# Loading x, k and v rows in longer runs and reordering the weight folds at the start of a gated attention/FFN kernel

## The chip, the cores and the metric

The kernel runs on one core of one Trainium2 chip. The metric is the device time of one execution in microseconds (us). All executions told here are of the state "fast", with a granted TensorE clock of 0.998 to 1.0 in the run records.

## The reference

```python
def reference(x, wqkv, w_phi, wo, w_gate, w_up, w_down, gate_w):   # cut: names of A and B merged
    g = sigmoid((x * gate_w).sum(-1, keepdims=True))
    # a: linear attention with softmax features, 32 heads of 20
    q, k, v = split(x @ wqkv)                       # x [2048, 640], wqkv [640, 1920]
    pq, pk = q @ w_phi[h], k @ w_phi[h]             # per head, 20 x 20
    phi_q = concat(softmax(pq), softmax(-pq)); phi_k = the same of pk
    kv, z = phi_k^T v, sum(phi_k)                   # over all rows
    a = (phi_q kv / (phi_q z + 1e-6)) @ wo
    b = (gelu(x @ w_gate) * (x @ w_up)) @ w_down    # inner width 1728
    return g * a + (1 - g) * b
```

## The kernel before

The rows of x are worked on in 16 tiles of 128; four tiles make a block. The kernel does not compute k and then multiply it by w_phi. It folds w_phi into the weights first: `wk2 = Wk * blockdiag(w_phi)`, and the same for q. For this it needs Wk and Wq transposed (`wkT`, `wqT`). Wk is transposed on TensorE. Wq is transposed by six DMA-transpose loads. Only the first four tiles of x pass through this start; from tile 4 on a steady loop runs, whose first instruction is the first v projection with 512 columns. I call it **the full projection** and use its start time as the milestone for everything that comes before.

Two words recur. A bank is one of the eight pieces (0 to 7) of the memory into which matmuls write their results. An eviction is the copy of a bank's content into a weight or data tile by VectorE or ScalarE; until it is done, the program lets no later matmul write that bank.

The loads (cut):

```python
xload(0, "sp"); xload(2, "act"); xload(1, "sp"); xload(3, "act")     # x of block 0, one tile each
for kt in range(KD):                                                  # v rows, five loads
    sc.dma("sp", ... self.wvk[:, kt, 0:D] <- w3[:, kt, 2*D:3*D], writes=[("wv", kt)])
sc.dma("act", ... wphi ...)                                           # 640 runs of 40 bytes
sc.dma("sp", ... self.wk_raw <- w3[:, :, D:2*D], writes=["wk_raw"])   # k rows, one load
sc.dma("sp", gload, writes=["wgate"])                                 # gate_w as a column: 640 runs of 2 bytes
for g, (h0, nh) in enumerate(self.GH):                                # six transposed loads of Wq
    sc.dma("sp", ... dma_start_transpose(self.wqT[:, g, :], ...),
           reads=["wk_raw"] if g == 0 else [], writes=[("wqT", g)])
xblock(1); xblock(2); xblock(3)                                       # transposed x of the other blocks
# ... FFN weights follow
```

One fold is six small matmuls and one eviction, by VectorE ("d") or ScalarE ("a"):

```python
def fold(self, kt, which, banks, ekey):
    for g, (h0, nh) in enumerate(self.GH):
        # matmul into banks[h0 // 16], reads ("w%sT" % which, g) and the block diagonal
    # one copy of both banks to wk2[kt] or wq2[kt] by VectorE or ScalarE

def pq(self, b, i, n):          # q projection: 5 matmuls into bank 6 + n % 2, the kt-th reads wq2[kt]
```

The order of the start (cut):

```python
for t, ek in enumerate("adad"): self.x_transpose(t, 4 + t, ek)     # banks 4..7
self.v_first({... blockdiag and first k transposes inside ...})    # v of tiles 0..3
self.w_transposes("k", (2, 3, 4, 5), (0, 6, 7, 0), "dadd")
for kt, (bk, ek) in enumerate(zip((6, 1, 4, 6, 0), "adada")):
    self.fold(kt, "k", (bk, bk + 1), ek)
self.k_early(0, 2)                    # k projection of tile 0, banks 2 and 3
self.k_early(1, 4)
self.fold(0, "q", (6, 7), "d"); self.fold(1, "q", (0, 1), "a")
self.k_early(2, 2)
self.fold(2, "q", (6, 7), "d"); self.fold(3, "q", (0, 1), "a"); self.fold(4, "q", (6, 7), "d")
self.k_norm(0)                        # softmax normalisation of k tile 0, VectorE
self.k_early(3, 4)
self.k_norm(1)
self.pq(0, 1, 1); self.pq(0, 0, 0); self.pq(0, 3, 3)
self.gram(0)                          # phi_k^T v of tile 0
self.k_norm(2)
self.pq(0, 2, 2)
# steady loop: vk(t), k_norm(t), gram, pq for t = 4..15, then the FFN
```

The softmax here doesn't subtract the row's maximum and nothing guards it: scores larger than these inputs give would overflow.

## Time and profile before

| | us |
|---|---|
| timed executions beside the first profile | 307.12, 307.26, 307.62 |
| the profiled execution itself | 306.63 |
| its span | 304.70 |
| first v matmul / first q fold / first q projection / full projection | 6.93 / 20.39 / 25.46 / 30.96 |

In the lines of the profile PE is TensorE, PEld its weight loads, DVE VectorE, ACT ScalarE, POOL GpSimd and SP SyncE, which sends out most loads (SPq is its queue); L345 is line 345 of that kernel's file. The head and the engine line of the page of the kernel before (busy time, share of the span, instructions):

```profile
span 304.7 us, 5022 instructions
...
PE 298.0 (98%) x2011; PEld 175.3 (58%) x2011; DVE 160.0 (53%) x312; ACT 106.8 (35%) x189; POOL 29.8 (10%) x59
```

TensorE is the limit. In this trace a fold matmul has a length of 0.21 us while the next one starts 0.05 us after it, so gaps of 0.15 us and less do not show as idle time; I count from start to start. The next lines are TensorE's waits in the kernel before between 4 and 32 us (engine, what was waiting, what released it: total us, times, longest).

```profile
PE ps L345 <- DVE wq_50 L358: 0.7, 1, 0.7
PE ps L376 <- DMA wvk<-in_A_wqkv_dram: 0.6, 1, 0.6
PE ps L488 <- ACT Eq L494: 0.3, 1, 0.3
PE ps L345 <- ACT wvk L360: 0.3, 1, 0.3
PE ps L365 <- DVE wvk L358: 0.2, 1, 0.2
```

TensorE waits for the first v rows, and several times for evictions that free a bank or deliver folded weights. These are lines of the timeline of the kernel before (start, length, engine, line, operation, count; in brackets the idle time before it and its releaser):

```profile
10.63 8.33 SPq L227 DMA_TRANSPOSE wqT<-in_A_wqkv_dram  x6
...
20.39 0.77 PE L345 MATMUL ps<-BD,wqT 120*128 120x120 bf16 x12
21.00 1.53 PE L365 MATMUL ps<-wvk,xT 128*128 128x384 bf16 x10
22.36 0.76 PE L345 MATMUL ps<-BD,wqT 120*128 120x120 bf16 x12
23.80 0.46 PE L345 MATMUL ps<-BD,wqT 120*128 120x120 bf16 x6 [0.68 <-DVE wq_50 L358]
24.10 1.53 PE L365 MATMUL ps<-wvk,xT 128*128 128x384 bf16 x10
25.46 2.32 PE L488 MATMUL ps<-xT,wq_50 128*128 128x512 bf16 x10
28.12 1.25 PE L488 MATMUL ps<-xT,wq_50 128*128 128x512 bf16 x5 [0.34 <-ACT Eq L494]
```

### The profile page before, as it was taken

Reading aid. Unit: us, or ns where it says so; the run is one execution under the profiler, and the core shown is the slowest. Engines: PE = TensorE matmul, PEld = TensorE weight load, DVE = VectorE, ACT = ScalarE, POOL = GpSimd, SP = SyncE. Lnnn points to the kernel's source line nnn. Section 1 sums busy time; section 2 is a strip of 40 time slices with the busy share of each in tenths; the row PEclk is TensorE's granted clock in tenths of the full one; section 3 lists DMA queues with packets and bytes.
Section 4 is the critical chain, followed back from the end, with each engine's and each line's share of the span. In section 5 each row is a group of like instructions: output and inputs, shape, how many; then the busy total and the mean of one; then the engine's idle time right before and its main releaser. Section 6 shows DMA issues by size and latency. Waiting matters only on the chain.

```text
span 304.7 us, 5022 instructions
## 1 busy us (share of the span) xinstructions
PE 298.0 (98%) x2011; PEld 175.3 (58%) x2011; DVE 160.0 (53%) x312; ACT 106.8 (35%) x189; POOL 29.8 (10%) x59
## 2 busy tenths in 40 slices
PE   7998999999999999999999999999999999999996
PEld 4664565655555555677545567754457764545763
DVE  1438999586775877234367710435770044567000
ACT  3388666667674222111322211123221122222111
POOL 7100000000000011111011000101110010111000
PEclk9999999999999999999999999999999999999999
DMA  7589996000000011120120111011111001110401
GB/s 222 140 150 209 369 369 221 0 2 0 2 0 0 2 22 24 24 65 25 43 20 4 22 24 43 24 43 23 17 6 44 24 26 41 22 22 0 45 22 45
DMA packets 34641, 18.29 MB, mean 60 GB/s; under 512 B 25850, under 2 KB 34618, under 8 KB 34618
## 3 DMA queue, kind: packets, MB, share of 16 engines
q1 hardware_dynamic: 33680, 17.62, 22.8%
q10 hardware_dynamic: 938, 0.35, 0.4%
q8 instruction: 16, 0.26, 0.4%
q14 instruction: 7, 0.06, 0.1%
HBM read 9.78 MB, written 2.62 MB: 41 GB/s over the span
## 4 chain that ended last, share of the span: by engine, by line
PE 94%; DMA 2%; ACT 1%; DVE 1%; issue 0%; SPq 0%; ACTq 0%; DVEq 0%
PE ps L572 37%; PE ps L654 20%; PE ps L365 12%; PE ps L660 7%; PE ps L488 6%; PE ps L609 4%; PE ps L462 4%; PE ps L376 2%; DMA wvk<-in_A_wqkv_dram 2%; PE ps L582 1%; PE ps L345 1%; ACT Eq L494 1%; PE ps L327 0%; ACT Ek L423 0%; DVE wkT L334 0%
## 5 line engine op out<-in xcount | busy, mean ns | idle before, releaser
L572 PE MATMUL ps<-xT,wu_sb 128*128 128x512 bf16 x260 | 64.6, 379 | 0.2 <-ACT Eq L494 0.2
L572 PE MATMUL ps<-xT,wg_sb 128*128 128x512 bf16 x260 | 64.6, 379 | 0.0
L654 PE MATMUL ps<-wd_sb,hT 128*128 128x320 bf16 (+2 forms) x448 | 63.8, 299 | 0.0
L575 ACT ACTIVATE gl<-ps 128x512 bf16<-128x512 f32 x52 | 31.1, 597 | 83.2 <-PE ps L572 81.0
L577 DVE TENSOR_TENSOR hT<-ps,gl 128x512 bf16<-128x512 f32 x52 | 35.7, 688 | 42.9 <-PE ps L572 42.9
L654 PEld LDWEIGHTS ps<-wd_sb,hT 128*128 128x128 bf16 x448 | 43.1, 98 | 18.2 <-DVE hT L577 0.4
L572 PEld LDWEIGHTS ps<-xT,wu_sb 128*128 128x128 bf16 x260 | 25.4, 98 | 31.1 <-issue 0.7
L365 PE MATMUL ps<-wvk,xT 128*128 128x512 bf16 (+2 forms) x220 | 40.6, 335 | 0.2 <-DVE wvk L358 0.2
L572 PEld LDWEIGHTS ps<-xT,wg_sb 128*128 128x128 bf16 x260 | 24.9, 98 | 26.9
L670 ACT ACTIVATE outsb<-ps,Gm 128x640 bf16<-128x640 f32 (+2 forms) x17 | 13.0, 763 | 74.1 <-PE ps L660 74.1
L638 POOL TENSOR_TENSOR Og<-O_59,O_60 128x640 bf16<-128x640 bf16 x16 | 22.3, 1396 | 167.8 <-DVE O_60 L636 167.8
L365 PEld LDWEIGHTS ps<-wvk,xT 128*128 128x128 bf16 x220 | 21.1, 97 | 19.5 <-DVE wvk L358 0.6
L434 DVE TENSOR_REDUCE Dk<-Ek 128x64 f32<-128x1280 bf16 x16 | 23.7, 1482 | 10.0 <-ACT gcol L426 10.0
L625 DVE RECIPROCAL RH<-ps 128x32 f32<-128x32 f32 x16 | 5.7, 358 | 43.9 <-PE ps L609 42.8
L443 DVE TENSOR_TENSOR Ek<-Ek,Dk 128x640 bf16<-128x640 bf16 x32 | 25.0, 822 | 0.5
L488 PE MATMUL ps<-xT,wq_50 128*128 128x512 bf16 x100 | 24.7, 378 | 0.3 <-ACT Eq L494 0.3
L660 PE MATMUL ps<-wo_sb,goT 128*128 128x320 bf16 (+2 forms) x160 | 24.5, 299 | 0.0
L494 ACT ACTIVATE Eq<-ps 128x512 bf16<-128x512 f32 x40 | 21.8, 607 | 5.4 <-PE ps L488 5.4
L423 ACT ACTIVATE Ek<-ps 128x640 bf16<-128x640 f32 x32 | 20.7, 703 | 2.2 <-PE ps L365 2.2
L660 PEld LDWEIGHTS ps<-wo_sb,goT 128*128 128x128 bf16 x160 | 15.5, 98 | 6.3
L609 PEld LDWEIGHTS ps<-KV,Eq 128*128 128x128 bf16 x192 | 12.0, 98 | 3.1
L609 PE MATMUL ps<-KV,Eq 128*128 128x154 bf16 x192 | 13.7, 221 | 0.0
(68 smaller groups left out, 178.7 us busy)
## 6 DMA issues: line engine op xcount, KB each, us to landing
out_dram<-outsb SPq DMA_DIRECT2D x15, 160.0 KB, 1.8
wd_sb<-in_B_w_down_dram SPq DMA_DIRECT2D x1, 2080.0 KB, 12.7
wg_sb<-in_B_w_gate_dram SPq DMA_DIRECT2D x1, 1120.0 KB, 7.0
wu_sb<-in_B_w_up_dram SPq DMA_DIRECT2D x1, 1120.0 KB, 9.5
wg_sb<-in_B_w_gate_dram SPq DMA_DIRECT2D x1, 960.0 KB, 9.0
wu_sb<-in_B_w_up_dram SPq DMA_DIRECT2D x1, 960.0 KB, 9.4
wvk<-in_A_wqkv_dram SPq DMA_DIRECT2D x5, 160.0 KB, 4.8
wk_raw<-in_A_wqkv_dram SPq DMA_DIRECT2D x1, 800.0 KB, 6.5
```

The costliest lines, as they stand in the source:

```text
L365: sc.op("pe", lambda e, kt=kt: e.matmul(self.bank(bank)[:, bcol:bcol + n], self.xT[:, kt, t * P:(t + 1) * P], self.wvk[:, kt, c0:c0 + n], ...
L434: sc.op("dve", lambda e: e.tensor_reduce(self.Dk[:, se, 0, :].rearrange("p (s h) -> p s h", h=H), self.Ek[:, se, :, :].rearrange("p s (h d ...
L443: sc.op("dve", lambda e, v=v, r=r: e.tensor_tensor(v, v, r, ALU.mult), reads=[("Rk", se)], writes=[("Ek", se, s)])
L488: sc.op("pe", lambda e, kt=kt: e.matmul(self.bank(bank), self.wq2[:, kt, i * P:(i + 1) * P], self.xT[:, kt, b * self.BT:(b + 1) * self.BT] ...
L494: sc.op("act", lambda e, s=s, scale=scale: e.activation(self.Eq[:, s, i, b * self.BT:(b + 1) * self.BT], self.bank(bank), AF.Exp, scale=sc ...
L572: sc.op("pe", lambda e, kt=kt, w=w, bk=bk: e.matmul(self.bank(bk), w[:, kt, c * P:(c + 1) * P], xs(kt), start=(kt == 0), stop=(kt == self. ...
L575: sc.op("act", lambda e: e.activation(self.gl[:, slot, :], self.bank(banks[0]), AF.Gelu_apprx_tanh), reads=[("ps", banks[0])], writes=[("g ...
L577: sc.op("dve", lambda e: e.tensor_tensor(self.hT[:, c, :], self.bank(banks[1]), self.gl[:, slot, :], ALU.mult), reads=[("ps", banks[1]), ( ...
L609: sc.op("pe", lambda e, s=s, i=i, n=n, o0=o0, k0=k0, bk=bk, r=r: e.matmul(self.bank(bk)[:, o0:o0 + n], self.Eq[:, s, i, t * P:(t + 1) * P] ...
L638: sc.op("pool", lambda e: e.tensor_tensor(self.Og[:, sl, :], self.O1[:, sl, :], self.O2[:, sl, :], ALU.add), reads=[("O", 0, sl), ("O", 1, ...
L654: sc.op("pe", lambda e: e.matmul(self.bank(bk, w), self.hT[:, c, tt * P:(tt + 1) * P], self.wd_sb[:, c, w0:w0 + w], start=(c == 0), stop=F ...
L660: sc.op("pe", lambda e: e.matmul(self.bank(bk, w), self.goT[:, gs, k, :], self.wo_sb[:, k, w0:w0 + w], start=False, stop=(k == self.KD - 1 ...
```

## The change

Its intent is to fill TensorE's gaps at the start. Loads: x of block 0 goes in two loads of two tiles (2560-byte runs; the rows of block 0 are dealt out differently, and its stores follow); k and v rows come as one run per k-slice; the gate column comes as one row and is turned by five tiny matmuls. Order: v steps and k transposes interleaved differently, k folds over three bank pairs with k of tile 0 between them, q folds between the k tiles and all evicted by VectorE.

```diff
-        xload(0, "sp"); xload(2, "act"); xload(1, "sp"); xload(3, "act")        # condensed
-        for kt in range(KD): ... wvk[:, kt, 0:D] <- v rows
-        ... wk_raw <- k rows; gload (gate column)
+        xload(2, "act")                               # tiles 2 and 3
+        sc.dma("act", ... wphi ...); sc.dma("act", ... gw_row ...)
+        xload(0, "sp")                                # tiles 0 and 1
+        for kt in range(KD): ... w3[:, kt, 0:2*D] <- k and v rows, writes=[("wv", kt), ("wk", kt)]
@@ order
+        warm(7); xt(0, 6, "a"); xt(1, 7, "d"); warm(2); xt(2, 6, "a"); xt(3, 7, "d")
+        vs(0, 0); vs(1, 0); self.gate_column(3); vs(2, 0); vs(3, 0)
+        ... v steps, blockdiag, k transposes tk(0..5) between the last v steps ...
+        self.fold(0, "k", (6, 7), "d")
+        self.fold(1, "k", (4, 5), "a")
+        self.fold(2, "k", (2, 3), "d")
+        ks(0, 0)                                      # k of tile 0, one k-slice
+        self.fold(3, "k", (6, 7), "a")
+        ks(0, 1)
+        self.fold(4, "k", (4, 5), "d")
+        ks(0, 2); ks(0, 3); ks(0, 4)
+        self.k_evac(0, 0)
+        self.k_early(1, 2)
         self.fold(0, "q", (6, 7), "d")
-        self.fold(1, "q", (0, 1), "a")
-        self.k_early(2, 2)
+        self.fold(1, "q", (0, 1), "d")
+        self.k_early(2, 4)
         self.fold(2, "q", (6, 7), "d")
-        self.fold(3, "q", (0, 1), "a")
+        self.fold(3, "q", (0, 1), "d")
+        self.k_early(3, 2)
         self.fold(4, "q", (6, 7), "d")
         self.k_norm(0)
-        self.k_early(3, 4)
         self.k_norm(1)
         self.pq(0, 1, 1)
```

(Several calls stand on one line here; the cuts are marked.)

More of the change, by code (lines that the diff above doesn't have):

```diff
@@ L157, in alloc @@
         self.zero = T("zero", [P, 512], BF16)
+        self.gw_row = T("gw_row", [1, D], BF16)
+        self.one = T("one", [1, 1], BF16)
         self.gcol = T("gcol", [P, NT], F32)
@@ L186, in alloc @@
         place([
-            [("wvk", [P, KD, 2 * D + 2], BF16), ("wq2", [P, KD, D], BF16)],
+            [("w3", [P, KD, 3 * D + 2], BF16), ("wq2", [P, KD, D], BF16)],
             [("hT", [P, NFC, BT], BF16), ("gl", [P, 3, BT], BF16)],
@@ L190, in alloc @@
         place([
-            [("xtok", [P, self.TB, D], BF16), ("wk_raw", [P, KD, D], BF16),
-             ("wkT", [P, 6, D], BF16), ("wqT", [P, 6, D], BF16), ("wq_raw", [P, KD, D], BF16)],
+            [("xtok", [P, self.TB, D], BF16), ("wkT", [P, 6, D], BF16), ("wqT", [P, 6, D], BF16)],
             [("goT", [P, 6, KD, P], BF16), ("O1", [P, 2, D], BF16), ("O2", [P, 2, D], BF16),
@@ L208, in loads @@
         w3 = self.wqkv.rearrange("(kt p) n -> p kt n", p=P)
-        def gload(e):
-            with nc.allow_non_contiguous_dma(reason="gate_w as a column"):
-                return e.dma_start(self.wvk[:, :, 2 * D:2 * D + 1], self.gw.rearrange("(kt p o) -> p kt o", p=P, o=1))
-        def xload(t, q):
-            sc.dma(q, lambda e: e.dma_start(self.xtok[:, t, :], self.x[t * P:(t + 1) * P, :]), writes=[("xtok", t)])
-        xload(0, "sp")
+        x4 = self.x[0:self.BT, :].rearrange("(p j) n -> p j n", j=self.TB)
@@ L216, in loads, with xload, kvload @@
+        def xload(j, q):
+            sc.dma(q, lambda e: e.dma_start(self.xtok[:, j:j + 2, :], x4[:, j:j + 2, :]),
+                   writes=[("xtok", j), ("xtok", j + 1)])
+        def kvload(kt):
+            sc.dma("sp", lambda e: e.dma_start(self.w3[:, kt, 0:2 * D], w3[:, kt, D:3 * D]), writes=[("wv", kt), ("wk", kt)])
         xload(2, "act")
-        xload(1, "sp")
-        xload(3, "act")
-        for kt in range(KD):
-            sc.dma("sp", lambda e, kt=kt: e.dma_start(self.wvk[:, kt, 0:D], w3[:, kt, 2 * D:3 * D]), writes=[("wv", kt)])
@@ L221, in loads @@
         sc.dma("act", lambda e: e.dma_start(self.wphi_sb[:, :].rearrange("d (h f) -> d h f", f=DH),
                                             self.wphi.rearrange("h d f -> d h f")), writes=["wphi"])
-        sc.dma("sp", lambda e: e.dma_start(self.wk_raw[:, :, :], w3[:, :, D:2 * D]), writes=["wk_raw"])
-        if self.QDMA:
-            sc.dma("sp", gload, writes=["wgate"])
-            for g, (h0, nh) in enumerate(self.GH):
-                sc.dma("sp", lambda e, g=g, h0=h0: e.dma_start_transpose(
-                    self.wqT[:, g, :], self.wqkv[:, h0 * DH:h0 * DH + P]),
-                    reads=["wk_raw"] if g == 0 else [], writes=[("wqT", g)])
-        else:
-            sc.dma("sp", lambda e: e.dma_start(self.wq_raw[:, :, :], w3[:, :, 0:D]), writes=["wq_raw"])
-            sc.dma("sp", gload, writes=["wgate"])
+        sc.dma("act", lambda e: e.dma_start(self.gw_row[0:1, :], self.gw.rearrange("(o n) -> o n", o=1)), writes=["gw_row"])
@@ L234, in xblock @@
+        xload(0, "sp")
+        for kt in range(KD):
+            kvload(kt)
+        for g, (h0, nh) in enumerate(self.GH):
+            sc.dma("sp", lambda e, g=g, h0=h0: e.dma_start_transpose(
+                self.wqT[:, g, :], self.wqkv[:, h0 * DH:h0 * DH + P]),
+                reads=[("wk", KD - 1)] if g == 0 else [], writes=[("wqT", g)])
         def xblock(b, after=()):
@@ L237, in xblock @@
                 reads=after, writes=[("xT", t) for t in range(b * 4, b * 4 + 4)])
-        xblock(1, [] if self.QDMA else ["wq_raw"])
+        xblock(1)
         xblock(2)
@@ L317, in blockdiag, with wk_transposes @@
             reads=rd, writes=["BD"])
-    def w_transposes(self, which, gs, banks, ekeys):
+    def wk_transposes(self, gs, banks, ekeys):
         sc = self.sc
-        raw, T = (self.wk_raw, self.wkT) if which == "k" else (self.wq_raw, self.wqT)
         for g, b, ek in zip(gs, banks, ekeys):
@@ L327, in w_transposes, with gate_column @@
                 sc.op("pe", lambda e, kt=kt: e.transpose(
-                    pv[0:rows, kt * P:(kt + 1) * P], raw[:, kt, h0 * self.DH:h0 * self.DH + rows], self.ident[:, :]),
-                    reads=["w%s_raw" % which, "ident"], writes=[("ps", b)], signal=(kt == self.KD - 1))
-            dst = T[0:rows, g, :]
+                    pv[0:rows, kt * P:(kt + 1) * P], self.w3[:, kt, h0 * self.DH:h0 * self.DH + rows],
+                    self.ident[:, :]),
+                    reads=[("wk", kt), "ident"], writes=[("ps", b)], signal=(kt == self.KD - 1))
+            dst = self.wkT[0:rows, g, :]
             src = pv[0:rows, 0:self.D]
-            wr = [("w%sT" % which, g)]
             if ek == "d":
-                sc.op("dve", lambda e: e.tensor_copy(dst, src), reads=[("ps", b)], writes=wr)
+                sc.op("dve", lambda e: e.tensor_copy(dst, src), reads=[("ps", b)], writes=[("wkT", g)])
             else:
-                sc.op("act", lambda e: e.activation(dst, src, AF.Copy), reads=[("ps", b)], writes=wr)
+                sc.op("act", lambda e: e.activation(dst, src, AF.Copy), reads=[("ps", b)], writes=[("wkT", g)])
+    def gate_column(self, b):
+        sc = self.sc
+        for kt in range(self.KD):
+            sc.op("pe", lambda e, kt=kt: e.matmul(
+                self.bank(b)[:, kt:kt + 1], self.gw_row[0:1, kt * P:(kt + 1) * P], self.one[0:1, 0:1],
+                start=(kt == 0), stop=(kt == self.KD - 1), skip_group_check=True),
+                reads=["gw_row", "one"], writes=[("ps", b)], signal=(kt == self.KD - 1))
+        sc.op("dve", lambda e: e.tensor_copy(
+            self.w3[:, :, 3 * self.D:3 * self.D + 1], self.bank(b, self.KD).unsqueeze(2)),
+            reads=[("ps", b)], writes=["wgate"])
     def fold(self, kt, which, banks, ekey):
@@ L350, in fold @@
         if which == "k":
-            dst = self.wvk[:, kt, self.D:2 * self.D]
+            dst = self.w3[:, kt, 2 * self.D:3 * self.D]
         else:
@@ L365, in proj @@
             sc.op("pe", lambda e, kt=kt: e.matmul(
-                self.bank(bank)[:, bcol:bcol + n], self.xT[:, kt, t * P:(t + 1) * P], self.wvk[:, kt, c0:c0 + n],
+                self.bank(bank)[:, bcol:bcol + n], self.xT[:, kt, t * P:(t + 1) * P], self.w3[:, kt, self.D + c0:self.D + c0 + n],
                 start=(kt == 0), stop=(kt == self.KD - 1)),
@@ L369, in proj, with v_step, k_step @@
                 writes=[("ps", bank)], signal=(kt == self.KD - 1))
-    def v_first(self, extra):
+    def v_step(self, t, kt):
         sc = self.sc
-        for kt in range(self.KD):
-            for t in range(4):
-                for c0, n, bk, col in ((0, 480, t, 0), (480, 160, 4 + t // 3, 160 * (t % 3))):
-                    sc.op("pe", lambda e, kt=kt, t=t, c0=c0, n=n, bk=bk, col=col: e.matmul(
-                        self.bank(bk)[:, col:col + n], self.xT[:, kt, t * P:(t + 1) * P], self.wvk[:, kt, c0:c0 + n],
-                        start=(kt == 0 and col == 0), stop=(kt == self.KD - 1), skip_group_check=True),
-                        reads=[("xT", t), ("wv", kt)], writes=[("ps", bk)], signal=(kt == self.KD - 1))
-                for f in extra.get((kt, t), ()):
-                    f()
+        for c0, n, bk, col in ((0, 480, t, 0), (480, 160, 4 + t // 3, 160 * (t % 3))):
+            sc.op("pe", lambda e, c0=c0, n=n, bk=bk, col=col: e.matmul(
+                self.bank(bk)[:, col:col + n], self.xT[:, kt, t * P:(t + 1) * P], self.w3[:, kt, self.D + c0:self.D + c0 + n],
+                start=(kt == 0 and col == 0), stop=(kt == self.KD - 1), skip_group_check=True),
+                reads=[("xT", t), ("wv", kt)], writes=[("ps", bk)], signal=(kt == self.KD - 1))
+    def k_step(self, t, kt):
+        sc = self.sc
+        for c0, n, bk, col in ((640, 384, 2 * t, 128), (1024, 257, 2 * t + 1, 0)):
+            sc.op("pe", lambda e, c0=c0, n=n, bk=bk, col=col: e.matmul(
+                self.bank(bk)[:, col:col + n], self.xT[:, kt, t * P:(t + 1) * P], self.w3[:, kt, self.D + c0:self.D + c0 + n],
+                start=(kt == 0), stop=(kt == self.KD - 1)),
+                reads=[("xT", t), ("wk2", kt), "wgate"], writes=[("ps", bk)], signal=(kt == self.KD - 1))
     def v_first_evac(self, ts, ek, tail):
@@ L510, in attention_state @@
         order = [(b, i) for b in range(self.NB) for i in range(self.KD)]
-        self.sc.op("dve", lambda e: e.memset(self.zero[:, :], 0.0), writes=["zero"])
-        for i in range(self.NWARM):
-            self.sc.op("pe", lambda e: e.matmul(self.bank(3), self.zero[:, 0:P], self.zero[:, :], start=True, stop=True),
-                       reads=["zero"], writes=[("ps", 3)])
-        for t, ek in enumerate("adad"):
-            self.x_transpose(t, 4 + t, ek)
-        tk = lambda g, b, ek: (lambda: self.w_transposes("k", (g,), (b,), ek))
@@ L518, in attention_state @@
-        ve = lambda ts, ek, tail=False: (lambda: self.v_first_evac(ts, ek, tail))
-        self.v_first({(1, 3): [lambda: self.blockdiag((6, 7))],
-                      (4, 0): [ve([0], "a")],
-                      (4, 1): [tk(0, 6, "d"), ve([1], "a")],
-                      (4, 2): [tk(1, 7, "d"), ve([2], "a")]})
-        self.w_transposes("k", (2, 3, 4, 5), (0, 6, 7, 0), "dadd")
-        ve([0, 1, 2], "a", True)()
-        ve([3], "a")()
-        ve([3], "a", True)()
-        for kt, (bk, ek) in enumerate(zip((6, 1, 4, 6, 0), "adada")):
-            self.fold(kt, "k", (bk, bk + 1), ek)
@@ L529, in attention_state, with warm @@
-        self.k_early(0, 2)
-        self.k_early(1, 4)
+        sc = self.sc
+        sc.op("dve", lambda e: e.memset(self.zero[:, :], 0.0), writes=["zero"])
+        sc.op("dve", lambda e: e.memset(self.one[:, :], 1.0), writes=["one"])
+        def warm(n):
+            for i in range(n):
+                sc.op("pe", lambda e: e.matmul(self.bank(3), self.zero[:, 0:P], self.zero[:, :], start=True, stop=True),
+                      reads=["zero"], writes=[("ps", 3)])
+        vs, ve, xt = self.v_step, self.v_first_evac, self.x_transpose
@@ new lines, in attention_state @@
+        tk = lambda g, b, ek: self.wk_transposes((g,), (b,), ek)
+        warm(7)
+        xt(0, 6, "a")
+        xt(1, 7, "d")
+        warm(2)
+        xt(2, 6, "a")
+        xt(3, 7, "d")
+        vs(0, 0)
+        vs(1, 0)
+        self.gate_column(3)
+        vs(2, 0)
+        vs(3, 0)
+        for t in range(4):
+            vs(t, 1)
+        self.blockdiag((6, 7))
+        for kt in (2, 3):
+            for t in range(4):
+                vs(t, kt)
+        tk(0, 6, "d")
+        tk(1, 7, "a")
@@ new lines, in attention_state @@
+        vs(0, 4)
+        ve([0], "a", False)
+        vs(1, 4)
+        tk(2, 6, "d")
+        ve([1], "a", False)
+        vs(2, 4)
+        tk(3, 7, "d")
+        ve([2], "a", False)
+        vs(3, 4)
+        tk(4, 0, "d")
+        tk(5, 1, "d")
+        ve([0, 1, 2], "a", True)
+        ve([3], "a", False)
+        ve([3], "a", True)
+        ks = self.k_step
+        self.fold(0, "k", (6, 7), "d")
+        self.fold(1, "k", (4, 5), "a")
+        self.fold(2, "k", (2, 3), "d")
+        ks(0, 0)
@@ L531, in attention_state @@
+        self.fold(3, "k", (6, 7), "a")
+        ks(0, 1)
+        self.fold(4, "k", (4, 5), "d")
+        ks(0, 2)
+        ks(0, 3)
+        ks(0, 4)
+        self.k_evac(0, 0)
+        self.k_early(1, 2)
         self.fold(0, "q", (6, 7), "d")
-        self.fold(1, "q", (0, 1), "a")
-        self.k_early(2, 2)
+        self.fold(1, "q", (0, 1), "d")
+        self.k_early(2, 4)
         self.fold(2, "q", (6, 7), "d")
-        self.fold(3, "q", (0, 1), "a")
+        self.fold(3, "q", (0, 1), "d")
@@ L595, in num @@
         DB, DH = self.DB, self.DH
-        old = [("xtok", k) for k in range(4)] + ["wk_raw"] + [("wkT", g) for g in range(6)] + [("wqT", g) for g in range(6)] + ["wq_raw"]
+        old = [("xtok", k) for k in range(4)] + [("wkT", g) for g in range(6)] + [("wqT", g) for g in range(6)]
         parts = {0: [(0, 0, 6), (1, 6, 12), (2, 12, 15)], 1: [(2, 16, 19), (3, 19, 25), (4, 25, 31)]}
@@ L671, in evac @@
                   reads=[("ps", k) for k in bks] + ["Gm"], writes=[("outsb", os_, w)for w in ((0, 320) if n == 640 else (w0,))])
-            sc.dma("sp", lambda e: e.dma_start(self.out[t * P:(t + 1) * P, w0:w0 + n], self.outsb[:, os_, w0:w0 + n]),
+            rows = self.out[t * P:(t + 1) * P, :]
+            if t < self.TB:
+                rows = self.out[0:self.BT, :].rearrange("(p j) n -> p j n", j=self.TB)[:, t, :]
+            sc.dma("sp", lambda e: e.dma_start(rows[:, w0:w0 + n], self.outsb[:, os_, w0:w0 + n]),
                    reads=[("outsb", os_, w) for w in ((0, 320) if n == 640 else (w0,))], writes=[("out", t, w0)])
@@ L686 @@
     NUMB = 2
-    NWARM = 7
-    QDMA = True
-    oldw = [(w, k) for w in ("wv", "wk2", "wq2") for k in range(5)] + ["wgate"]
+    oldw = [(w, k) for w in ("wk", "wv", "wk2", "wq2") for k in range(5)] + ["wgate"]
     def ffn(self):
```

## The prediction

> **What bounds the kernel now.** TensorE: 298.0 of 304.7 us busy (engine table), 94% of the chain of waits. From 31 us on (windows view) it has practically no gap; that stretch is untouched but for the row order of block 0's stores, which nothing waits for. So only the first 31 us count. There the timeline has these TensorE gaps: 0.6 us before the first v matmul (6.93 us), which waits for the first v rows (issued 1.72, landed 6.80); and waits for evictions: 0.3 + 0.3 us in the k folds, 0.2 before k of tile 0, 0.68 before the last q fold, 0.34 before the third q projection. Busy spans contain the pipeline's tail; by start-to-start times I count about 2.9 us lost from 12.35 us on. That is all the change can win: 1%.
>
> **What changes, costed by the trace.**
> 1. Loads: same bytes, in 2560-byte runs instead of 1280; a 1280-byte packet takes 55 ns, a 1792-byte one 74, so a few per cent faster. But v's first step now needs a run twice as long. I expect it to land at 6.9 +- 0.4 us: v starts where it did. The Trainium skill ("DMA: Bandwidth & Descriptors", Queues, rings and completion order) says that the two issuing queues use the same 16 engines; so two queues for x save issue time only (0.4 us per issue here).
> 2. The gate column, a DMA that nothing waited for, becomes five tiny matmuls: about 0.3 us of TensorE, plus 0.15 because bank 3 must be evicted before v of tile 3. Cost 0.45.
> 3. K weight transposes: the last two evictions (0.49 us each) both run on VectorE, so the first k fold waits about 0.75 us (before: 0.55). Fold 1 waits 0.1.
> 4. K projection of tile 0 between folds: the evictions (0.82 VectorE, 0.72 ScalarE) are longer than the matmuls between them (fold 0.30, k step 0.27): waits of about 0.45, 0.2 and 0.4 us. K of tile 1 ends about 0.3 us later, relative to the first k transpose.
> 5. Q folds: the 0.68 us wait goes. But the last q fold now comes after k of tile 3, on banks 6 and 7, and the first q projection writes bank 7 right behind it. It waits for that eviction: 0.26 (hand-over, as in the trace) + 0.82 + 0.06 = about 1.15 us, which k of tile 3 hid before.
> 6. VectorE starts the first k normalisation about 1.4 us later; gram of tile 0 waits about 0.1. Later grams have over 2 us of slack.
>
> Sum: -2.9 removed, +3.45 new waits, +0.45 gate, 0 at the start: +1.0 us at the first full v/k projection (30.96 us before). The rest shifts with it. As the order looks tuned by measurement, and v may start some tenths earlier, I shade this to +0.75.
>
> **Predicted: 308.0 us, range 306.8 to 309.0.** Faster by over 2%: 0.01; within 2%: 0.98; slower by over 2%: 0.01.
>
> **What would show it.** Right: v starts at 6.7 to 7.3 us; the first q projection has about 1.1 us of TensorE idle, released by VectorE's copy of the folded q weights; the first 512-column v projection starts near 32.0 us; from there the length equals before's. Wrong: no such wait; v starting below 6.5 us; the full projection before 31.0.
>
> **What would make it wrong.** The first k/v run landing a microsecond early or late; the one-row gate load landing late (it sits behind 640 short w_phi packets) and holding v; a clock that rises later because TensorE idles while x lands; weight loads slowing the mixed folds.

## The result, and the profile after

The changed kernel took 306.95 us (median of four; 306.58 to 307.05), the kernel before 307.25 us. The ratio is 0.9986, with a 95% interval of 0.9969 to 1.0003. A ratio is the mean time of one kernel's fast runs over that of the other's of the same rounds, so it is not quite the ratio of the medians. A later repeat in five rounds gave 0.9985 (0.9973 to 0.9998). So the change gains about 0.15%: half a microsecond by the means, 0.3 us by the medians. The first interval alone does not exclude no gain; the repeat just does. The prediction had called the verdict (within 2%), and the range held the time, by 0.15 us at its lower edge. That was in part luck: it had expected a loss of 0.75 us, and the sign was wrong.

The page's head and engine line of the changed kernel:

```profile
span 305.1 us, 5006 instructions
...
PE 297.3 (97%) x1992; PEld 175.1 (57%) x2018; DVE 162.2 (53%) x317; ACT 105.2 (34%) x186; POOL 29.8 (10%) x59
```

Its span is *longer* than that of the profile before (305.1 against 304.7) although its times are shorter. The waits of TensorE between 4 and 32 us:

```profile
PE ps L499 <- DVE wq_50 L365: 1.2, 1, 1.2
PE ps L389 <- DVE w_49 L365: 0.4, 2, 0.3
PE ps L352 <- DVE wkT L330: 0.2, 1, 0.2
```

And the lines of the timeline that answer to those shown of before, in order of time:

```profile
9.31 8.46 SPq L227 DMA_TRANSPOSE wqT<-in_A_wqkv_dram  x6
...
20.95 0.74 PE L352 MATMUL ps<-BD,wqT 120*128 120x120 bf16 x12
21.53 1.53 PE L372 MATMUL ps<-w_49,xT 128*128 128x384 bf16 x10
22.89 0.74 PE L352 MATMUL ps<-BD,wqT 120*128 120x120 bf16 x12
23.48 1.53 PE L372 MATMUL ps<-w_49,xT 128*128 128x384 bf16 x10
24.84 0.45 PE L352 MATMUL ps<-BD,wqT 120*128 120x120 bf16 x6
26.51 3.46 PE L499 MATMUL ps<-xT,wq_50 128*128 128x512 bf16 x14 [1.21 <-DVE wq_50 L365]
29.80 0.83 PE L473 MATMUL ps<-vaug,Ek 128*128 128x147 bf16 x12
```

The wait before the last q fold (0.68 us) is gone. In its place stands a wait of 1.21 us, 1.38 from start to start, before the first q projection: it writes bank 7, and the last fold sits on bank 7 until VectorE has copied it. That is step 5 of the prediction as written. The full projection starts at 31.56 us, 0.60 us *later* than in the profile before (the prediction said 1.0). Yet the timed runs are half a microsecond faster. So the two profiles and the two sets of times disagree, and that is what the experiments had to settle. The second visible change is in the first line: the transposed Wq loads go out at 9.31 instead of 10.63 us.

### The profile page after: what moved, and what is told of

Same layout as the page of the kernel before. It is cut to its first block, busy times and chain, and to the rows that moved or that the text cites. A ratio compares the mean times of both kernels' runs of the same rounds, so it can differ in the third digit from the quotient of the medians.

```text
span 305.1 us, 5006 instructions
## 1 busy us (share of the span) xinstructions
PE 297.3 (97%) x1992; PEld 175.1 (57%) x2018; DVE 162.2 (53%) x317; ACT 105.2 (34%) x186; POOL 29.8 (10%) x59
## 4 chain that ended last, share of the span: by engine, by line
PE 95%; DMA 1%; DVE 1%; issue 1%; ACT 1%; ACTq 0%; DVEq 0%
PE ps L619 36%; PE ps L701 20%; PE ps L372 12%; PE ps L707 7%; PE ps L499 7%; PE ps L656 4%; PE ps L473 4%; PE ps L381 2%; PE ps L629 1%; DMA xtok<-in_A_x_dram 1%; PE ps L352 1%; PE ps L288 1%; ACT Eq L505 1%; DVE w_49 L365 1%; PE ps L323 0%
## 5 line engine op out<-in xcount | busy, mean ns | idle before, releaser
L619 PE MATMUL ps<-xT,wg_sb 128*128 128x512 bf16 x251 | 62.8, 379 | 0.3
L372 PE MATMUL ps<-w_49,xT 128*128 128x512 bf16 (+2 forms) x210 | 39.0, 337 | 0.1
L372 PEld LDWEIGHTS ps<-w_49,xT 128*128 128x128 bf16 x210 | 20.2, 97 | 18.8
L499 PE MATMUL ps<-xT,wq_50 128*128 128x512 bf16 x91 | 23.4, 378 | 1.7 <-DVE wq_50 L365 1.2
L499 PEld LDWEIGHTS ps<-xT,wq_50 128*128 128x128 bf16 x100 | 8.6, 97 | 9.2 <-DVE wq_50 L365 1.1
```

The lines of the kernel that those rows point to most:

```text
L372: sc.op("pe", lambda e, kt=kt: e.matmul(self.bank(bank)[:, bcol:bcol + n], self.xT[:, kt, t * P:(t + 1) * P], self.w3[:, kt, self.D + c0:s ...
L499: sc.op("pe", lambda e, kt=kt: e.matmul(self.bank(bank), self.wq2[:, kt, i * P:(i + 1) * P], self.xT[:, kt, b * self.BT:(b + 1) * self.BT] ...
L619: sc.op("pe", lambda e, kt=kt, w=w, bk=bk: e.matmul(self.bank(bk), w[:, kt, c * P:(c + 1) * P], xs(kt), start=(kt == 0), stop=(kt == self. ...
```

## The experiments

In all that follows, a milestone is read from the trace of one execution, and a ratio is against the kernel before of the same rounds.

### Null test: the kernel before again

No edit.

> The kernel before, unchanged, once more: a null test that also gives a second trace of it. Theory A (the profiled execution of before was a lucky one: it took 306.63 us where its timed runs took 307.12 to 307.62): the trace from the first full v/k projection (30.96 us) to the last matmuls is the same to 0.02 us, and the differences between executions lie before it (when the first v rows land, when the clock rises) or in the last store. The new execution then has that projection at 31.0 to 31.9 us. Theory B (the middle varies): the start stays at 30.96 and the rest differs. Ratio 1.000 within 0.001.

Measured: ratio 0.9999 (0.9986 to 1.0012), single times 306.92 to 307.78 us. The traced execution took 307.77 us, and its full projection started at 32.08 us: 1.12 us later than in the first trace, and later than I had said. From there to the end of the span it is the same to 0.01 us: 304.70 - 30.96 = 273.74 and 305.82 - 32.08 = 273.74. So theory A holds: the middle is fixed, the start differs. Where it differs, this trace of the kernel before says:

```profile
10.94 9.10 SPq L227 DMA_TRANSPOSE wqT<-in_A_wqkv_dram  x6
...
20.39 0.72 PE L345 MATMUL ps<-BD,wqT 120*128 120x120 bf16 x5
21.77 0.50 PE L345 MATMUL ps<-BD,wqT 80*128 80x80 bf16 x7 [0.66 <-DMA wqT<-in_A_wqkv_dram]
22.10 1.53 PE L365 MATMUL ps<-wvk,xT 128*128 128x384 bf16 x10
```

Up to the first q fold at 20.39 us the two executions agree to 0.01 us from the first k transpose (12.35 us) on. Then the fold waits, for its fifth and its sixth matmul, until 21.77 us. The last transposed load had landed at 21.72 us. In the first trace it landed at 20.61 us and the sixth matmul started at 20.66, 0.07 us after the fifth. The kernel before has a wait that its first profile does not show, because in that execution the loads came almost in time.

### The changed kernel again

No edit.

> The changed kernel, unchanged, once more, for a tighter ratio and a second trace. If the profiled pair is typical (full projection at 31.56 against 30.96 us), the ratio is 1.002. If before's profiled execution was lucky by about 0.6 us, the ratio is 0.998 to 1.000. Its own start should vary less than before's, because its v step waits for TensorE's own transposes and not for a transfer: projection at 31.5 to 31.7 us in this trace.

Measured: 306.84 us, ratio 0.9985 (0.9973 to 0.9998). In this trace the full projection starts at 31.27 us, outside the 31.5 to 31.7 that I had expected. Its TensorE clock rose at 4.4 us instead of 6.1; the first ten x transposes took 0.73 instead of 1.25 us, and v started at 6.56 instead of 6.85 us. So the changed kernel's start varies too, by another cause. The last Wq load landed at 20.03 us; the sixth fold matmul came at about 20.9 us. There is no wait for it, nor in the first trace (landed 19.39, used at about 21.2).

### The last q fold on other banks

```diff
         self.k_early(3, 2)
-        self.fold(4, "q", (6, 7), "d")
+        self.fold(4, "q", (4, 5), "d")
```

> The changed kernel with its last q fold on banks 4 and 5 instead of 6 and 7, so the first q projection need not wait for that eviction to free bank 7; only its fifth matmul still needs the evicted weights. Theory A (the 1.3 us wait before the first q projection is on the path): its first matmul starts at 25.1 instead of 26.5 us, the full projection about 0.85 us earlier (30.7), ratio to before lower by 0.003. Theory B (VectorE binds: the normalisation of k tile 0 starts after that same eviction, at 26.1 us, takes 3.7 us, and gram of tile 0 must wait for it until 29.8 us): the first q projection starts at 25.1, but gram of tile 0 still starts at 29.8 and the full projection at 31.5 to 31.6; no gain. I expect B.

Measured: 306.69 us, ratio 0.9978 (0.9966 to 0.9990). The interval includes the changed kernel's 0.9985. The timeline of this run:

```profile
25.31 3.75 PE L499 MATMUL ps<-xT,wq 128*128 128x512 bf16 x14
29.08 0.37 PE L473 MATMUL ps<-vaug,Ek 128*128 128x147 bf16 x3
29.82 0.65 PE L473 MATMUL ps<-vaug,Ek 128*128 128x63 bf16 x9 [0.37 <-DVE Ek L454]
```

The q projection begins 1.2 us earlier, as theory B said it would, and the time is not gained: gram of tile 0 now begins at 29.08 us, stops after three matmuls, and waits until 29.82 us for VectorE's normalisation. In the changed kernel it ran at 29.80 us. The full projection starts at 31.39 us, against 31.56 and 31.27. The reason is visible on VectorE, in the changed kernel's timeline:

```profile
25.40 0.82 DVE L365 CAST wq_50<-ps 128x640 bf16<-128x640 f32 x1 [0.39 <-PE ps L352]
26.14 1.48 DVE L445 TENSOR_REDUCE Dk<-Ek 128x64 f32<-128x1280 bf16 x1
27.65 0.55 DVE L449 RECIPROCAL Dk<-Dk 128x64 f32<-128x64 f32 x1
28.24 1.56 DVE L454 TENSOR_TENSOR Ek<-Ek,Dk 128x640 bf16<-128x640 bf16 x2
```

The same eviction (first line) gates two things: the q projection, and VectorE's own next job, whose last part ends at 29.80 us. Freeing TensorE from the first leaves it waiting for the second.

### The same, and gram of tile 0 behind the fourth q projection

```diff
         self.pq(0, 3, 3)
+        self.pq(0, 2, 2)
         self.gram(0)
         self.k_norm(2)
-        self.pq(0, 2, 2)
```

(with the edit of the run before)

> As the one before, and the fourth q projection moved ahead of gram of tile 0, so that TensorE has work while VectorE normalises. If VectorE's chain was what ate the gain, the full projection now starts at 30.7 to 30.9 us, 0.7 to 0.9 us earlier than in the changed kernel, and the ratio falls by 0.0025. If the wait for bank 7 itself was all, this does no better than the one before.

Measured: 305.75 us, ratio 0.9951 (0.9939 to 0.9963), full projection at 30.62 us. Against the changed kernel the ratio falls by 0.0034, a little more than expected. From the first k transpose to the full projection this trace takes 18.51 us, against 19.37 in both traces of the changed kernel and 19.24 with the bank edit alone. So the wait before the first q projection costs about 0.86 us, and nearly all of it is gained only when TensorE is also given other work while VectorE normalises. The move of gram without the bank edit was not run; in the changed kernel gram shows no wait that it could remove.

### The loads of the change with the order of before

```diff
 # against the changed kernel, condensed
-        warm(7); xt(0, 6, "a"); xt(1, 7, "d"); warm(2); xt(2, 6, "a"); xt(3, 7, "d")
+        warm(7); x transposes on banks 4, 5, 6, 7
-        ... the changed order of v steps, k transposes, k folds, k steps and q folds ...
+        ... the order of before, to the letter ...
-        gw_row load and gate_column(3)
+        the gate column by its DMA, between the k/v rows and the Wq loads
```

> The changed kernel's loads of x and of the k/v runs, with the order of work of before (x transposes on four bank pairs, k folds, q folds and evictions as before; the gate column by its DMA as before). My theory now: in before, the first q fold waits for the last transposed load of q weights, by 0.1 us in the first trace and 0.9 us in the second; those six loads go out one by one behind the k rows, and the new loads let them start at 9.3 instead of 10.6 to 10.9 us. So here the last one lands by 19.6 us, the first q fold (near 19.9 us) never waits, v starts near 6.4 us, the full projection starts at 30.4 to 30.6 us, and the ratio is 0.996 to 0.997, better than the changed kernel's 0.9985. Rival (the new order is what gains): the ratio stays at 1.000 here.

Measured: 305.75 us, ratio 0.9954 (0.9940 to 0.9967); all five runs lie between 305.57 and 306.08 us. This is better than I expected (0.996 to 0.997), and better than the whole change by 0.31%, about 1 us. V starts at 6.01 us, the last Wq load lands at 19.68 us, and the first q fold runs through, in this run's timeline:

```profile
19.67 0.74 PE L356 MATMUL ps<-BD,wqT 120*128 120x120 bf16 x12
20.25 1.53 PE L376 MATMUL ps<-w,xT 128*128 128x384 bf16 x10
```

The full projection starts at 30.22 us. The slack is small here: the sixth matmul came about 0.2 us after the landing.

### The order of the change with the loads of before

```diff
 # against the changed kernel, condensed
-        x in two loads of two tiles; k and v rows in one run; gw_row and gate_column(3)
+        x in four loads of one tile; five v loads, one k load; the gate column by its DMA behind them
```

> The other half: loads as before (x by tile, v rows, then all k rows, gate column by its DMA), with the changed kernel's order of folds, k steps and q projections, and without the gate matmuls. My theory: the q weights again start at 10.6 us or later and land at 20.6 to 21.8 us, so the first q fold (near 20.6) waits 0 to 1.1 us in some executions; the new order's own wait of about 1.3 us before the first q projection is there; full projection at 31.2 to 32.2 us; ratio 1.000 to 1.002. Rival (the new order gains): 0.998 or less.

Measured: 307.31 us, ratio 1.0002 (0.9990 to 1.0015), full projection at 31.37 us. The Wq loads go out at 10.74 us, the last lands at 20.96 us, and the wait is back, in this run's timeline:

```profile
20.19 0.41 PE L358 MATMUL ps<-BD,wqT 120*128 120x120 bf16 x5
21.00 0.50 PE L358 MATMUL ps<-BD,wqT 80*128 80x80 bf16 x7 [0.40 <-DMA wqT<-in_A_wqkv_dram]
```

Together with the run before, this splits the change: the loads gain 0.46% when they stand alone, the order alone gains nothing. In the whole change part of the loads' gain is lost again. Two parts of the start cost most of it: x is transposed over two banks instead of four, with two warming matmuls between (v starts at 6.56 to 6.85 us instead of 6.01; the clock, which rose at different times, may have a share in this), and the gate matmuls add 0.31 us (from the first v matmul to the first k transpose it takes 5.34 us with them, and 5.03 us in the two runs that have the same order without them).

### K and v rows apart again, and the gate column by DMA again

First edit, on the changed kernel:

```diff
-        w3[:, kt, 0:2 * D] <- k and v rows of slice kt          # five loads
+        w3[:, kt, D:2 * D] <- v rows of slice kt                # five loads
+        w3[:, :, 0:D]      <- all k rows                        # one load
```

> The changed kernel with k and v rows loaded apart again (five v loads, then one k load, 1280-byte runs), all else as changed. If the longer runs are what makes the k rows land early, the q weights start at 10.0 us or later instead of 9.3; if it is the gate column's 640 two-byte packets, gone in this kernel too, they start by 9.6. The time should be the changed kernel's within 0.1 us either way, because the first q fold comes at 20.9 us and has over 0.8 us of slack: ratio 0.998 to 0.999.

Second edit, on the changed kernel:

```diff
-        gw_row load; gate_column(3)
+        gload(gate column, 640 two-byte runs) between the k/v rows and the Wq loads
```

> The changed kernel with the gate column loaded by its DMA again, in the place it had before (behind the k rows, ahead of the q weights), and the five gate matmuls gone. The gate matmuls and the wait for bank 3 take 0.37 to 0.45 us between the second and third v tile in the traces; all of it is on TensorE's path, so the full projection comes 0.35 to 0.45 us earlier than the changed kernel's (31.2 or 30.9 us) unless the q weights, pushed back by the gate's short packets, then bind: ratio 0.997 to 0.9975.

Measured: 306.78 us, ratio 0.9985 (0.9972 to 0.9997), and 306.86 us, ratio 0.9986 (0.9973 to 0.9998). The first is as expected. The Wq loads go out at 9.56 and 9.72 us, within the 9.3 to 9.8 us of the other kernels with the new loads. So neither the long k/v run nor the missing gate packets *alone* makes these loads early. The second missed its forecast: its trace has the full projection at 30.88 us, as expected, but its times are no better than the changed kernel's. The traced execution was the fastest of its five (306.52 us). Why the other four do not show the 0.3 us is open; a Wq landing that varies with only some 0.7 us of slack is a guess.

### The gate column's DMA later, in the kernel before

```diff
-            sc.dma("sp", gload, writes=["wgate"])                    # right behind the k rows
+        sc.dma("pool", gload, reads=["wk_raw"], writes=["wgate"])    # after they have landed
```

> The kernel before with one line moved: the gate column's DMA (640 two-byte packets) goes out on GpSimd's queue after the k rows have landed, instead of on the load queue right behind them. In both traces of before those packets cut into the last 100 KB of the k rows and the transposed q weights start at 10.6 and 10.9 us. Theory: the k rows land 0.5 us or more earlier, the q weights start by 10.1 us, the first q fold waits no more or less than 0.3 us, and the ratio falls to 0.998. Rival (the q weights are not what holds before in its typical execution): the ratio stays at 1.000.

Measured: 306.84 us, ratio 0.9990 (0.9972 to 1.0007). This is inconclusive. The k rows landed at 10.42 us, only 0.2 us earlier than in the first trace of before (0.5 us earlier than in the second), and the Wq loads went out at 10.44 us, not by 10.1, so the edit hardly did what it was meant to do; the q fold still waited 0.4 us for the Wq load. The two-byte packets are a small part of it.

What then makes the new loads early? The packets' records in the traces give the megabytes that had arrived by 7 and by 8 us:

| x of block 0 | kernel | k and v rows | gate packets | MB by 7 us | MB by 8 us | Wq loads go out, us |
|---|---|---|---|---|---|---|
| four loads | before, two traces | apart | yes | 1.53, 1.55 | 1.86, 1.90 | 10.63, 10.94 |
| four loads | before, gate later | apart | later | 1.54 | 1.87 | 10.44 |
| four loads | order only | apart | yes | 1.59 | 1.91 | 10.74 |
| two loads | k and v apart | apart | no | 1.70 | 2.07 | 9.56 |
| two loads | loads only, gate by DMA, and the next two runs | one run | yes | 1.71 to 1.78 | 2.10 to 2.19 | 9.30 to 9.74 |
| two loads | changed (two traces) and its two bank runs | one run | no | 1.64 to 1.75 | 2.05 to 2.15 | 9.31 to 9.77 |

The rows fall into two groups, and what divides them is the loading of x in two loads instead of four (with it the w_phi load, 640 packets of 40 bytes, goes second instead of third on its queue). The closest pair is "gate later" and "k and v apart": in both the k and v rows are loaded apart and no gate packets stand before the Wq loads, and the k rows landed at 10.42 and 9.54 us. The single k/v run adds nothing that stands out. With one x load fewer ahead of it the k load also goes out earlier, at 3.68 instead of 4.11 us. No run undid the x loads alone, so this is a comparison across runs, and whether the longer runs of x, the earlier issue or the place of w_phi does it is open.

### Two moves on top of the loads, and the changed kernel repaired

First, on the loads-only kernel:

```diff
-        self.fold(4, "q", (6, 7), "d")
-        self.k_norm(0)
         self.k_early(3, 4)
+        self.fold(4, "q", (2, 3), "d")
+        self.k_norm(0)
         self.k_norm(1)
@@ and the fourth q projection ahead of gram of tile 0, as above
```

> The kernel of the loads-only run with two moves: the last q fold after k of tile 3 but on banks 2 and 3, which no q projection writes, and the fourth q projection ahead of gram of tile 0. The wait of 0.65 us before the last q fold goes; the first q projection waits about 0.2 us at its fifth matmul. Full projection at 29.7 to 29.9 us instead of 30.22, ratio 0.9935 to 0.9945. If VectorE's later normalisation binds instead, gram of tile 0 waits and nothing is gained: 0.9954.

Second, on the changed kernel with the edits of the second bank run:

```diff
-        xt(0, 6, "a"); xt(1, 7, "d"); warm(2); xt(2, 6, "a"); xt(3, 7, "d")
+        xt(0, 4, "a"); xt(1, 5, "d"); xt(2, 6, "a"); xt(3, 7, "d")
-        gw_row load; gate_column(3)
+        gload(gate column) between the k/v rows and the Wq loads
```

> The changed kernel with all repairs: last q fold on banks 4 and 5, fourth q projection ahead of gram of tile 0, gate column by DMA, and x transposed over four banks without the two warming matmuls between. Against the kernel with the first two repairs (full projection 30.62 us) v starts 0.5 to 0.7 us earlier and 0.3 us of gate matmuls go: full projection at 29.6 to 29.9 us if the q weights do not bind; they land near 19.8 us and the first q fold would come at 19.9, so up to 0.5 us may be lost in some executions. Ratio 0.993 to 0.995.

Measured: the first took 304.93 us, ratio 0.9926 (0.9910 to 0.9943), full projection at 29.70 us; the second 305.25 us, ratio 0.9939 (0.9922 to 0.9957), full projection at 29.44 us. Both beat both kernels. The first gained slightly more than forecast; the two intervals overlap, so which of them is better is open. Both outputs were correct.

### The Wq loads held back in the changed kernel

```diff
-        six Wq loads; xblock(1); xblock(2); xblock(3)
+        xblock(1); six Wq loads; xblock(2); xblock(3)
```

> The changed kernel with the transposed load of x block 1 moved ahead of the six q weight loads on the same queue, which delays them by the 2.6 us that it takes to go out. Theory (the landing of the last q weights is a wait of its own that the changed kernel merely has slack for, 0.6 to 1.5 us): the last one lands at 22.0 to 22.4 us, the first q fold's last block waits 0.8 to 1.3 us for it, the full projection moves to 32.2 to 32.8 us, ratio 1.0015 to 1.0035. Rival (that landing does not matter): 0.9985, unchanged.

Measured: 308.31 us, ratio 1.0038 (1.0021 to 1.0055). The six issues began at 11.86 us, as forecast, but the last load landed at 23.12 us, later than I had said: one of the issues took 2.24 us, and the last load landed 3.75 us after its own issue, against 2.89 in the first trace of the changed kernel. This run's timeline:

```profile
21.19 0.42 PE L351 MATMUL ps<-BD,wqT 120*128 120x120 bf16 x5
23.16 0.50 PE L351 MATMUL ps<-BD,wqT 80*128 80x80 bf16 x7 [1.56 <-DMA wqT<-in_A_wqkv_dram]
```

The full projection moved to 33.53 us (expected 32.2 to 32.8). The rival is out: that landing is on the path as soon as the slack is used up. In five traces (before, before again, order only, gate later, and this one) the sixth matmul starts 0.04 to 0.05 us after the landing: 20.61/20.66, 21.72/21.77, 20.96/21.00, 20.87/20.92, 23.12/23.16.

## Why the prediction was right or wrong

The milestones, in us, side by side:

| | before, trace 1 | before, trace 2 | changed, trace 1 | changed, trace 2 |
|---|---|---|---|---|
| time of that execution | 306.63 | 307.77 | 307.03 | 306.59 |
| first v matmul | 6.93 | 6.75 | 6.85 | 6.56 |
| Wq loads go out / last one landed | 10.63 / 20.61 | 10.94 / 21.72 | 9.31 / 19.39 | 9.61 / 20.03 |
| first q fold | 20.39 | 20.39 | 20.95 | 20.66 |
| first q projection | 25.46 | 26.79 | 26.51 | 26.21 |
| full projection | 30.96 | 32.08 | 31.56 | 31.27 |
| from there to the end of the span | 273.74 | 273.74 | 273.53 | 273.53 |

**The bound, and that only the first 31 us count: right.** From the full projection to the end it takes 273.53 to 273.74 us in all traces. The 0.2 us between the two kernels there was not forecast; it lies at the very end. The last store is issued 271.21 to 271.22 us after the full projection in all 14 traces. Then SyncE runs through the program's closing waits for its loads and stores, one instruction after another; the program deals these transfers out over 16 semaphores in turn, and the closing waits go through them in a fixed order. Before, the first of these waits is the one for the last store, and ten more of about 0.06 us each follow. The changed kernel has 57 instead of 60 loads and stores on SyncE, so its last store falls on a semaphore three places away: three waits pass while the store is still under way, and seven follow. That is 3 x 0.06 = 0.19 us. The other traces agree: with 58 (loads only, for one) it takes 273.64 us from the full projection to the end, with 60 (order only) 273.72.

**Step 1, the loads: wrong in size and in consequence.** The first k/v run landed at 5.88 us, not at 6.9. That did not move v, because x landed 0.3 us later (first transpose at 4.54 instead of 4.22 us) and the transposes took until 6.85. But the k rows, and with them all that waits for them on the same queue, moved up: the Wq loads went out 1.3 us earlier. The prediction says "v starts where it did" and stops there. The remark on the two issuing queues missed the point: both kernels use two queues for x. What differs is the number of loads. That both queues share the same 16 engines, quoted there from the Trainium skill, is tested by no run here.

**Step 2, the gate matmuls: right in kind, too large.** 0.31 us instead of 0.45.

**Steps 3 and 4, the k folds: right.** Forecast waits of 0.75 + 0.1 + 0.45 + 0.2 + 0.4 = 1.9 us; measured start to start, 0.59 + 0.21 + 0.34 + 0.17 + 0.42 = 1.73 us. The interleaving of k steps and folds does not hide the evictions, because an eviction (0.82 or 0.72 us) is longer than what stands between.

**Step 5, the wait for bank 7: right.** Forecast 1.15 us, measured 1.38. The bank experiment adds what the prediction had only half seen in step 6: the same eviction also holds VectorE's normalisation, so taking away the wait alone gains nothing measurable. Step 6 had VectorE start that normalisation 1.4 us later; it started at 26.14 instead of 25.11 us, 1.19 us later when both are counted from the first k transpose.

**The sum: this is the step that failed.** "-2.9 removed, +3.45 new waits, +0.45 gate, 0 at the start" was counted from the first trace of before, and was then added to the median of its timed runs. Against that trace the changed kernel's full projection is indeed later, by 0.60 and 0.31 us in its two traces. But that trace was the luckiest execution of before seen by then (306.63 us; the timed runs took 307.12 to 307.62), and it stayed the second fastest of 42. The term that was missing is the wait of the first q fold for the last transposed Wq load: nearly nothing in the first trace, about 1.1 us in the second. The times put the typical execution of before in between: a median time of 307.25 us, less the 1.93 us by which time and span differed in its first profile, is a span of 305.32 us and so a full projection at about 31.6 us (an estimate from these numbers). The changed kernel does not have that wait in either trace. Its new waits therefore replace some 0.6 us of an old one, on average. That turns the loss at the full projection into a gain of 0.1 to 0.3 us (0.3 us by the medians, half a microsecond by the means, less the 0.2 us at the end). The rest of the gain is the 0.2 us of closing waits, which has nothing to do with what the change was meant for.

The Trainium skill describes such a stretch in "Perfetto Trace Analysis", What "DMA-bound" means: an issuing sequencer whose track is solid DMA slices is itself the bound. The trace agrees. SP is solid from 10.63 to 18.95 us with six issues of 1.27 us, one of them longer, while the DMA engines' mean busy share from 10.6 to 19 us is 0.61; by this reading these loads are bound by their issue, and an earlier start brings them forward. I had read that line and not asked when its last result is used.

**What is shown and what is not.** Shown: the wait for Wq (0.5 to 1.1 us from start to start in the second trace of before, in order only and in gate later, nearly nothing in the first trace of before, absent with the new loads, and back when they are held back); the 0.2 us of closing waits; that the new order alone gains nothing; that the wait for bank 7 and VectorE's normalisation hide each other. Not shown: that the times of before spread for this cause alone, since only two of its executions were traced (one later timed execution took 306.20 us, less than the first trace, so more than this wait varies); the effect of the x loads alone; and the missing gain of the gate-by-DMA run.

## What to carry to other kernels

Compare the time of the profiled execution with the timed ones before counting from its trace: when it is a lucky one, a wait that the typical execution has may show as nothing. Look for transfers that land just before their use, for they can be waits of the next execution, and when a change shortens a queue, follow everything behind it on that queue. Before removing a wait for an eviction, ask what else that eviction releases, and give the waiting engine other work in the same edit.

## What the Trainium skill lacked or had wrong

- "DMA: Bandwidth & Descriptors" (Latency and other measured facts) has a bandwidth for transposed loads, 261 GB/s in the non-contiguous case, but no issue time in us; elsewhere the page has only a count of sequencer cycles for small tiles. Here each transposed load of 160 KB took 1.27 us to go out from SP, and in every trace looked at one of the six took 1.6 to 2.6 us. By these issues that is at most 129 GB/s (163,840 bytes in 1.27 us), whatever the engines could move.
- The same page ("Why small descriptors are slow") speaks of about 3 cycles of fixed cost per packet. Here a 1280-byte packet took 55 ns and a 2560-byte one 102 ns (medians), which puts the fixed part at 8 ns (2 x 55 - 102; an estimate that takes the rest as proportional to the bytes).
- No page has a figure for what went with the number of loads here: with x of block 0 in two loads instead of four, 1.64 to 1.78 MB had arrived by 7 us instead of 1.53 to 1.59 MB.
- "TensorE: Matmul & The Clock Gate" (Part 1) puts the rise of the clock at about 4 us of activity, give or take 0.5 us between runs. The first matmul was at 1.26 us in these traces and the clock rose at 4.0 to 7.1 us in the twelve that recorded it, so 2.8 to 5.9 us later; the matmuls in between were not all back to back.
- "Perfetto Trace Analysis" does not say that the traced execution has to be placed among the timed ones: here it was 306.63 us against 307.12 to 307.62.
- No page has a cost for the waits on transfers with which a program like this ends: here they came 0.06 us apart, and the place of the last store's semaphore among them moved the end by 0.2 us.
